# Two of sixteen expert weights loaded as 24, 24 and 80 rows, with an eight-row transfer ahead of the first two parts

## The chip, the cores and the metric

The kernel runs on one core of one Trainium2 chip. A core has a matrix engine (PE, with its weight loads shown apart as PEld), a vector engine (DVE), a scalar engine (ACT), a general engine (POOL, GpSimd) and a queue engine (SP), and sixteen DMA engines that move data between the device memory and the core's own memory of 128 partitions (rows). The metric is the device time of one execution in microseconds, as the median of several runs. Lower is better.

## The reference

The reference is an attention layer, followed by a soft mixture of experts over its output. Batch is 4, heads are 8, the sequence is 768, a head has 64 columns. Three heads see the whole causal triangle, five see four sink positions and a window of 64.

```python
scores = np.where(mask, scale * q @ k.T, -1e9)
attn   = softmax(scores) @ v                    # 4 x 8 x 768 x 64
x      = attn.transpose(0, 2, 1, 3).reshape(3072, 512)

logits     = x @ phi                            # 3072 x 32
d          = softmax over the 3072 rows (logits)
slot_input = (d.T @ x).reshape(8, 4, 512)
for e in range(8):
    h = np.maximum(slot_input[e] @ w1[e], 0.0)  # w1[e] is 512 x 1024
    slot_out[e] = h @ w2[e]                     # w2[e] is 1024 x 512
c   = softmax over the 32 slots (logits)
out = c @ slot_out                              # 3072 x 512, float32
```

All inputs are float32. The sixteen weights (eight `w1`, eight `w2`) are 2.1 MB each, so 33.6 MB of the 52.5 MB that the kernel reads are weights.

## The kernel before, in words

The kernel keeps everything in bfloat16 on the core. Every load is a DMA that POOL issues and that casts float32 to bfloat16 on the way. `dma()` (line 329) makes each of them: it enters an "issue" operation for POOL and a "land" operation into a plan, puts every issue behind the one before it (`fifo`), and lets the issue of a transfer wait for the landing of the transfer eight places earlier (`chain[-8]`). A planner (`Plan`) then orders all operations on all engines by keys, tuned shifts and estimated durations, and the program is emitted in that order. POOL does little else than issue these loads: it makes tables at the start, copies `elg` once for each of three batches (line 801), and issues the first output stores (line 1017).

The loads go in this order: q, k and v of batch 0 in two parts each, with weight 0 behind them; q, k, v of batch 1; weights 1, 2; q, k, v of batch 2; weights 3, 4, 5; q, k, v of batch 3; weights 6 to 10; and last weights 11 to 15 into memory that the attention no longer needs. Weights 0 to 7 are `w1` of the experts, 8 to 15 are `w2`. A weight is a tile of 128 rows, 16 KB of float32 to a row; `load_w` (line 385) loads it in one transfer. The loads of q, k and v have 96 rows. Weights 14 and 15 come in two halves of their columns each (`load_half`, line 381), so that the left half of the output can start before the right halves are there. A slot of memory (`slots`, eleven of them) has to come free before the next load into it is issued; PE frees one by transposing a q, k or v.

Meanwhile PE, ACT and DVE run the attention: transposes (line 566), scores (line 599), exponentials on ACT (line 668), masks on DVE (line 615), the product with v (line 729). After it come the experts: the first product (`H`, line 904), a transpose (line 926), the second product (`W2`, line 942), and the output (`OM`, line 998; scaled on ACT and DVE in lines 1006 and 1008), stored by `store` (line 1017): the left halves of the first three row groups by POOL, all else by SP.

Before the first data are there, PE multiplies zeros: `zeros` (line 482) issues six matmuls of the tile `zt` (128 x 448) into a scores buffer, twice.

Of the kernel before, what the change touches and what calls it, by code (L numbers as in the profile page):

```python
# [11 lines left out]
BF16 = mybir.dt.bfloat16  # L12
# [3 lines left out]
PSUM = bass.MemoryType.PSUM  # L16
KB = 512
PAD = 16


class Buf:
# [130 lines left out]
def pe(ns, n=1):  # L152
    occ = ns * n / 1000.0
    return {"PE": (occ, occ + 0.27)}
# [61 lines left out]
def kernel(  # L216
# [13 lines left out]
    nc = tc.nc  # L230
    P = 128
# [3 lines left out]
    NS = moe_phi.shape[1]  # L235
# [4 lines left out]
    sb = ctx.enter_context(tc.tile_pool(name="sb", bufs=1))  # L240
# [4 lines left out]

    slots = [sb.tile([P, 8 * KB + 2 * PAD], BF16, name=f"slot{i}") for i in range(11)]
    qk_mem = [sb.tile([P, 12 * KB], BF16, name=f"qk{i}") for i in range(2)]
# [18 lines left out]
    rs = [sb.tile([P, 2, 6], F32, name=f"rs{i}") for i in range(2)]  # L266
    rrow = sb.tile([P, 24], F32, name="rrow")
    sum4 = sb.tile([P, NS], BF16, name="sum4")
    zt = sb.tile([P, 448], BF16, name="zt")
    emask = sb.tile([P, 2], F32, name="emask")  # L270
    rcs = sb.tile([P, 1], F32, name="rcs")
    cols = sb.tile([P, 1], BF16, name="cols")
# [18 lines left out]
    scb = [ps.tile([P, 2, 512], F32, name=f"sc{i}") for i in range(2)]  # L291
# [23 lines left out]
    def on(eng, occ, late=0.18):  # L315
        return {eng: (occ, occ + late)}
# [12 lines left out]
    def dma(name, nbytes, buf, dst, src, deps=()):  # L329
        if len(chain) >= 8:  # L330
            deps = list(deps) + [chain[-8]]
        iss = pl.op("issue " + name, on("POOL", 0.645, 1.4), -100, deps=list(deps) + [fifo[0]],
                    acq=[buf] if buf else [], lead=1.3, emit=lambda o: nc.gpsimd.dma_start(dst(), src))  # L333
        fifo[0] = iss
        took = nbytes / 425000.0
        chain.append(pl.op("land " + name, {"DMA": (took, took + 1.3 + min(2.1, 0.22 * len(chain)))}, -100, deps=[iss] + chain[-1:], lead=3.4))
        return chain[-1]
# [25 lines left out]
    wbuf = [Buf("S8") for _ in range(NW)]  # L363
    wland = [None] * NW
    late_mem = {}

    def w_mem(i):

        m = late_mem[i]() if i in late_mem else slots[wbuf[i].slot][:, :]
        return m.rearrange("p (h x) -> p h x", h=2)[:, :, 0:4 * KB]  # L370
# [14 lines left out]
    def load_w(i, deps=()):  # L385
        if i < NE:
            src = moe_w1[i].rearrange("(di h a) f -> di h (a f)", h=2, a=2)
        else:
            src = moe_w2[i - NE].rearrange("(fi h a) d -> fi h (a d)", h=2, a=4)
        wland[i] = dma(f"w{i}", 2 << 20, None if i in late_mem else wbuf[i],  # L390
                       lambda: w_mem(i), src, deps=deps)


    def tables(o):
# [32 lines left out]
    def head_flags(o, n):  # L427
        cp = nc.scalar.copy if o.eng == "ACT" else nc.gpsimd.tensor_copy
        for a, j0, j1 in ((1, 1, 4), (0, 0, 1)):
            cp(fmx[:, n, :, j0:j1, :].rearrange("p i j d -> p i (j d)"),  # L430
               thr[:, a, n::4].rearrange("p (i o) -> p i o", o=1).to_broadcast([P, 2, 66 * (j1 - j0)]))
# [48 lines left out]
    zfb = Buf("SC")  # L480

    def zeros(name, n, key, dep, took=0.43):
        def emit_z(o):
            for _ in range(n):
                nc.tensor.matmul(scb[zfb.slot][:, 0, 0:448], zt[:, 0:128], zt, start=True, stop=True)  # L485

        return pl.op(name, pe(1000 * took, n), key, deps=dep, acq=[zfb] if name == "ZF0" else [], rel=[zfb],
                     emit=emit_z, mode="full", mm=n)
# [15 lines left out]
    for n in range(4):  # L504
        o_fm[n] = pl.op(f"fm{n}", on("ACT", 0.65) if n == 0 else on("POOL", 0.9), -8 if n == 0 else T * n - 3.5,
                        deps=[o_fl], emit=lambda o, n=n: head_flags(o, n))
# [5 lines left out]
    def batch_loads(b):  # L512
        for x in "qkv":
            load_part(x, b)

    load_w(0)
    batch_loads(1)
    load_w(1)
    load_w(2)
    batch_loads(2)  # L520
    for i in (3, 4, 5):
# [67 lines left out]
    def evs(x, b, n):  # L589
        return ev[x, 0, n // 2] if b == 0 else ev[x, b]  # L590
# [15 lines left out]
    def mask_emit(b, n, g):  # L606
        def f(o):
            pT = pTs[PTb[b, n].slot]
            mh = msk[:, n::4, :]
            if g < 2:  # L610
                pT = pT[:, :, 1024 * g:1024 * (g + 1)].rearrange("p i (a c) -> p i a c", a=2)[:, :, :, 0:256]
                mh = mh[:, :, 256 * g:256 * g + 512].rearrange("p i (a c) -> p i a c", a=2)
            else:
                pT, mh = pT[:, :, 2048:2432], mh[:, :, 256:640]
            nc.vector.tensor_tensor(pT, pT, mh, op=ALU.mult)  # L615
        return f
# [5 lines left out]
    for b in range(B):  # L622
        for n in range(4):
# [29 lines left out]
            for kk, g in enumerate(range(5)):  # L653
# [19 lines left out]
                for m, gs in enumerate(MGROUPS):  # L673
                    if gs[-1] == g:
                        o_m = pl.op(f"MK.{p}.{m}", on("DVE", [0.605, 0.605, 0.47][m]), key + 0.3,
                                    deps=[expo[p, x] for x in gs] + [o_hm[n]], emit=mask_emit(b, n, m))
# [3 lines left out]
        for ns in ([(0, 1), (2, 3)] if b == 0 else [(0, 1, 2, 3)]):  # L680
            sc = Buf("SC")

            def emit_lx(o, b=b, sc=sc, ns=ns):
# [4 lines left out]
                      deps=list(dict.fromkeys(e for n in ns for x in "qk" for e in evs(x, b, n))),  # L688
# [14 lines left out]
    for b in range(B):  # L703
        for n in range(4):
# [5 lines left out]
            for i in iorder:  # L710
                deps, need = [v2e[p], vfo[p]], set()
# [7 lines left out]
                def emit_pv(o, b=b, n=n, p=p, i=i):  # L719
                    pT = pTs[PTb[b, n].slot]  # L720
                    vb = vbs[VBb[b].slot]
                    for h in range(2):
                        for j in range(i + 1):
# [3 lines left out]
                            else:  # L727
# [5 lines left out]
                             deps=list(dict.fromkeys(deps)) + ([last] if last else []),  # L733
# [8 lines left out]
            for i0, i1 in halves:  # L742
                part = f"{p}" if i1 - i0 == 6 else f"{p}.{i0}"

                def emit_nm(o, i0=i0, i1=i1, b=b, n=n, p=p):
# [9 lines left out]
                                 deps=[pvo[i1 - 1], XBb[b].op], acq=[XBb[b]] if n == 0 else [], rel=[PVb[p]],  # L755
# [94 lines left out]

    late_mem[11] = lambda: qk_mem[QTb[2].slot][:, 0:8 * KB + 2 * PAD]
    late_mem[12] = lambda: vx_mem[VBb[2].slot][:, 0:8 * KB + 2 * PAD]
    late_mem[13] = lambda: xv_mem[:, 0:8 * KB + 2 * PAD]
    late_mem[14] = lambda: pt_mem[:, 10 * KB * PTb[3, 2].slot:10 * KB * PTb[3, 2].slot + 8 * KB]
# [233 lines left out]
```

## Time and profile before

| what | value |
|---|---|
| median of 3 runs | 151.17 us (150.8 to 151.35) |
| the profiled execution's own time | 150.88 us |
| its span, first to last instruction | 149.1 us, so 1.78 us lie around the span |
| PE busy | 125.5 us (84%) |
| DVE busy | 109.1 us (73%) |
| ACT busy | 107.4 us (72%) |
| POOL busy | 33.1 us (22%) |
| software DMA queue (POOL's), share of 16 engines' span | 95.0% |
| read from and written to device memory | 52.50 MB and 6.29 MB |
| weights and inputs issued by POOL, one issue | 629 to 891 ns on POOL |
| last load issued, landed | 108.43 us, 131.52 us |
| granted PE clock, mean | 0.935 |

The page of the profile shows busy times by engine, then the span cut into 40 slices with a digit of busy tenths in each; the row DMA there is the mean over the sixteen DMA engines, and GB/s counts bytes as they are written on the core, so a load that casts from float32 reads twice that. The chain of waits goes back from the last instruction, step by step, to what released it. A stretch (a window of time) gives busy times, granted clock, DMA share and GB/s of that window alone; the packets there overlap a little, so that the DMA share of a full window comes out over 1. Beside these views, the trace holds for each transfer sixteen marks of its completion, one from each DMA engine, with their times; they tell how far apart the engines are, and carry no engine's number.

### The profile page before, as it was taken

How to read it: one execution, taken by the hardware profiler on the slowest of the kernel's cores; microseconds unless marked ns; L12 is line 12 of the kernel's file. 1: busy time of each engine (PE TensorE's matmuls, PEld its weight loads, DVE VectorE, ACT ScalarE, POOL GpSimd, SP SyncE). 2: the span in 40 equal slices, each digit the busy share in tenths (PEclk: the TensorE clock that was granted, in tenths of full speed). 3: DMA queues.
4: the chain of work that ended last, by engine and by line, in shares of the span. 5: the costliest groups of instructions: out<-in, count | busy, mean ns of one | idle time of the engine just before them, and what ended most of it. 6: DMA issues, size and time to landing. Idle time of an engine off the chain costs nothing.

```text
span 149.1 us, 5309 instructions
## 1 busy us (share of the span) xinstructions
PE 125.5 (84%) x2351; PEld 85.8 (58%) x2351; DVE 109.1 (73%) x232; ACT 107.4 (72%) x138; POOL 33.1 (22%) x58
## 2 busy tenths in 40 slices
PE   6799987996999999999999997999779994959100
PEld 1297665774776776877667775757565552634000
DVE  1897999966898988999899997998953130749500
ACT  3127899996779999999999997999913530738300
POOL 6996301111111001210210122050630000430000
PEclk9999999999599999999999999999968999586975
DMA  2999999999999999999999999999999999999995
GB/s 21 193 210 210 216 214 215 216 214 213 216 210 215 215 216 218 209 212 218 214 216 212 211 216 219 216 211 212 213 220 215 201 196 198 142 305 336 391 422 209
DMA packets 14263, 32.92 MB, mean 221 GB/s; under 512 B 1376, under 2 KB 7008, under 8 KB 13856
## 3 DMA queue, kind: packets, MB, share of 16 engines
q0 software_dynamic: 11536, 27.79, 95.0%
q1 hardware_dynamic: 2704, 4.79, 8.5%
q8 instruction: 18, 0.29, 0.7%
q14 instruction: 5, 0.04, 0.1%
HBM read 52.50 MB, written 6.29 MB: 394 GB/s over the span
## 4 chain that ended last, share of the span: by engine, by line
PE 48%; DMA 15%; DVE 11%; ACT 8%; issue 7%; POOL 3%; DVEq 1%; POOLq 0%; ACTq 0%
DMA qk<-in_moe_w_dram 15%; PE tr L566 13%; PE sc L599 11%; PE pv L729 11%; ACT pt L668 5%; PE tr L762 3%; PE bk L998 3%; DVE xv L750 2%; PE tr L632 2%; DVE pt L615 2%; PE sc L485 2%; DVE vx L322 1%; ACT qk L320 1%; DVE slot L1008 1%; DVE vf L647 1%
## 5 line engine op out<-in xcount | busy, mean ns | idle before, releaser
L668 ACT ACTIVATE pt<-sc 128x1024 bf16<-128x1024 f32 x80 | 77.4, 1047 | 4.9 <-PE sc L599 4.6
L599 PE MATMUL sc<-qk 64*128 64x128 bf16 (+3 forms) x288 | 32.1, 298 | 1.6 <-ACT pt L668 1.4
L615 DVE TENSOR_TENSOR pt<-pt,msk 128x1024 bf16<-128x1024 bf16 (+1 forms) x48 | 30.1, 639 | 1.5 <-ACT pt L668 1.1
L729 PEld LDWEIGHTS <-pt 128*128 128x128 bf16 x640 | 23.9, 98 | 6.8 <-issue 3.7
L729 PE MATMUL pv<-vx,pt 128*128 128x65 bf16 x352 | 26.9, 194 | 0.1
L566 PEld LDWEIGHTS <-slot 96*64 96x64 bf16 x768 | 20.1, 115 | 7.2 <-issue 5.3
L729 PE MATMUL pv<-vf,pt 128*128 128x65 bf16 x288 | 21.7, 196 | 0.9 <-DVE xv L750 0.9
L566 PE MATMUL tr<-ident,slot 96*64 96x96 bf16 x576 | 18.0, 212 | 1.3 <-issue 1.3
L322 DVE COPY qk<-tr 128x768 bf16<-128x768 bf16 x28 | 14.9, 549 | 4.0 <-PE tr L566 3.9
L599 PEld LDWEIGHTS <-qk 64*128 64x128 bf16 x288 | 11.5, 95 | 9.0 <-issue 3.3
L750 DVE TENSOR_TENSOR xv<-pv,rs 128x768 bf16<-128x768 f32 (+1 forms) x17 | 15.5, 910 | 0.6
L333 POOL DMA_DIRECT2D slot<-in_moe_w_dram x11 | 7.8, 707 | 26.6 <-PE tr L566 19.2
L1006 ACT ACTIVATE slot<-bk,rrow 128x256 f32<-128x256 f32 (+1 forms) x17 | 8.5, 548 | 3.6 <-PE bk L998 3.5
L762 PE MATMUL tr<-ident,xv 128*128 128x128 bf16 x96 | 8.8, 230 | 1.4 <-DVE xv L750 0.9
L1008 DVE TENSOR_SCALAR slot<-bk,rrow 128x256 f32<-128x256 f32 (+1 forms) x19 | 9.3, 561 | 0.6 <-PE bk L998 0.4
L762 PEld LDWEIGHTS <-xv 128*128 128x128 bf16 x96 | 6.2, 102 | 4.9 <-DVE xv L750 2.5
L632 PE MATMUL tr<-ident,xv 128*128 128x128 bf16 x96 | 8.2, 220 | 1.0 <-issue 0.9
L322 DVE COPY xT<-tr 128x768 bf16<-128x768 bf16 (+1 forms) x14 | 7.3, 525 | 2.3 <-PE tr L762 1.3
L998 PE MATMUL bk<-msk,expT 128*128 128x256 bf16 (+1 forms) x36 | 8.4, 413 | 0.7 <-DVE msk L983 0.7
L322 DVE COPY vx<-tr 128x768 bf16<-128x768 bf16 x13 | 7.1, 550 | 1.1 <-PE tr L632 1.0
L632 PEld LDWEIGHTS <-xv 128*128 128x128 bf16 x96 | 5.7, 97 | 3.0 <-issue 2.5
L1017 POOL DMA_DIRECT2D out_dram<-slot x4 | 2.8, 709 | 19.6 <-DVE slot L1008 19.5
(101 smaller groups left out, 152.1 us busy)
## 6 DMA issues: line engine op xcount, KB each, us to landing
slot<-in_moe_w_dram POOLq DMA_DIRECT2D x11, 1024.0 KB, 26.4
out_dram<-slot SPq DMA_DIRECT2D x3, 1024.0 KB, 6.6
slot<-in_q_dram POOLq DMA_DIRECT2D x3, 768.0 KB, 30.4
slot<-in_k_dram POOLq DMA_DIRECT2D x3, 768.0 KB, 32.7
slot<-in_v_dram POOLq DMA_DIRECT2D x3, 768.0 KB, 23.8
out_dram<-slot SPq DMA_DIRECT2D x3, 512.0 KB, 3.7
qk<-in_moe_w_dram POOLq DMA_DIRECT2D x1, 1024.0 KB, 21.3
vx<-in_moe_w_dram POOLq DMA_DIRECT2D x1, 1024.0 KB, 24.0
```

The lines of the kernel that those rows point to most:

```text
L322: nc.vector.tensor_copy(dst, src)
L566: nc.tensor.transpose(dst_, rv[:, i, 8 * c + s, :], idv)
L599: nc.tensor.matmul(scb[sc.slot][:, i, c:c + 128 * nb], kk, qq.rearrange("p b c -> p (b c)"), start=True, stop=True)
L615: nc.vector.tensor_tensor(pT, pT, mh, op=ALU.mult)
L632: nc.tensor.transpose(t[:, 128 * j:128 * (j + 1)], vT[:, 6 * n + j, :], ident)
L668: nc.scalar.activation(pTs[PTb[b, n].slot][:, :, 512 * g:512 * (g + 1)], scb[sc.slot], ACT.Exp, scale=scale)
L729: nc.tensor.matmul(pvb[:, h, 65 * i:65 * (i + 1)], lt, rhs, start=(j == 0), stop=(j == i))
L750: nc.vector.tensor_tensor(xo, pvw[:, :, :, 0:64], r.rearrange("p i (j o) -> p i j o", o=1).to_broadcast([P, 2, i1 - i0, 64]), op=ALU.mult)
L762: nc.tensor.transpose(t[:, 128 * i:128 * (i + 1)], xv[:, i, 128 * n:128 * (n + 1)], ident)
L998: nc.tensor.matmul(banks[bf.slot][:, 0:w], out_lhs(gi, r), slot_out[:, cs], start=True, stop=True)
L1006: nc.scalar.activation(d, banks[bf.slot][:, 0:w], ACT.Copy, scale=sc_)
L1008: nc.vector.tensor_scalar(d, banks[bf.slot][:, 0:w], sc_, None, op0=ALU.mult)
```

## The change

Weights 6 and 7 (the `w1` of experts 6 and 7) are no longer loaded in one transfer of 128 rows. Each is loaded in three: rows 0 to 23, rows 24 to 47, and rows 48 to 127. In front of each of the two small parts stands a transfer of eight rows of `moe_phi` (128 bytes each, cast to 64) into a new tile `few` that nothing reads. So each of the two weights becomes five transfers in the order 8, 24, 8, 24, 80 rows. The bytes of the weights are the same. The tile `zt` shrinks from 448 to 416 columns, which gives the 64 bytes to a row that `few` takes, and the zero matmuls write 416 columns. No other load, and no operation of the other engines, is edited; the order of PE, DVE and ACT stays as it was, and on POOL the `elg` copy that stood behind the issues of weights 6 and 7 now stands between the two.

```diff
+UNEVEN = {6: (0, 24, 0, 24, 80), 7: (0, 24, 0, 24, 80)}
...
-    zt = sb.tile([P, 448], BF16, name="zt")
+    zt = sb.tile([P, 416], BF16, name="zt")
+    few = sb.tile([8, NS], BF16, name="few")
...
     def load_w(i, deps=()):
...
-        wland[i] = dma(f"w{i}", 2 << 20, None if i in late_mem else wbuf[i],
-                       lambda: w_mem(i), src, deps=deps)
+        if i not in UNEVEN:
+            wland[i] = dma(f"w{i}", 2 << 20, None if i in late_mem else wbuf[i],
+                           lambda: w_mem(i), src, deps=deps)
+            return
+        rows, p0 = UNEVEN[i], 0
+        for x, n in enumerate(rows):
+            if n == 0:
+                dma(f"gap{i}.{x}", 1024, None, lambda: few, moe_phi[0:8, :])
+                continue
+            wland[i] = dma(f"w{i}.{p0}", n << 14, wbuf[i] if p0 == 0 else None,
+                           lambda p0=p0, n=n: w_mem(i)[p0:p0 + n], src[p0:p0 + n], deps=deps)
+            p0 += n
+        assert p0 == 128
...
-                nc.tensor.matmul(scb[zfb.slot][:, 0, 0:448], zt[:, 0:128], zt, start=True, stop=True)
+                nc.tensor.matmul(scb[zfb.slot][:, 0, 0:416], zt[:, 0:128], zt, start=True, stop=True)
```

## The prediction

> **What bounds the kernel now.** I read the page first (which resource is full), then the chain of waits at its end (what releases the last work), then stretches around that point (what the DMA engines do there), and POOL's timeline (what could hold the changed transfers up).
>
> ```profile
> DMA  2999999999999999999999999999999999999995
> q0 software_dynamic: 11536, 27.79, 95.0%
> q8 instruction: 18, 0.29, 0.7%
> ```
>
> The DMA engines are full from the second slice to the next to last: reading 33.6 MB of weights and 18.9 MB of q, k, v is what the time consists of. The queue of instruction fetches carries little, 18 packets, but each goes to one engine only.
>
> ```profile
> 107.56 0.86 POOL pt L333
> 108.43 23.09 DMA qk<-in_moe_w_dram
> 131.52 0.04 issue
> 131.56 0.43 PE bk L942 x8
> 132.09 0.49 DVE msk L983
> 132.63 3.91 PE bk L998 x16
> ```
>
> The last half weight is issued at 108.43 and lands at 131.52; PE goes on 0.04 us later. From there to the end of the span 17.6 us follow (second product, output, stores), so a landing that moves by x moves the end by x, as long as the half before it (weight 15, left) moves too, which releases the first stores.
>
> ```profile
> 124.00:126.00 2.00, 0.27 (x12) 0.09 (x1) 0.00 (x0) 0.00 (x0) 0.00 (x0) 1.00 1.45 197
> 127.60:128.00 0.40, 0.40 (x3) 0.30 (x2) 0.31 (x1) 0.00 (x0) 0.00 (x0) 0.50 0.77 102
> 128.00:128.80 0.80, 0.80 (x6) 0.58 (x4) 0.79 (x2) 0.74 (x2) 0.01 (x1) 0.50 0.80 102
> 128.90:129.90 1.00, 1.00 (x6) 0.59 (x4) 1.00 (x3) 1.00 (x4) 0.90 (x2) 0.53 0.65 89
> ```
>
> The last two columns are DMA share and GB/s. From 127.6 on the rate is half (102 against 197): half of the engines have finished while the others still load. The sixteen completion marks say the same:
>
> | transfer | earlier eight engines, us | later eight, us |
> |---|---|---|
> | weight 6 | 82.72 to 83.44 | 83.94 to 85.60 |
> | weight 15, left half | 122.30 to 122.69, and 123.53 | 124.68 to 125.22, and 126.25 |
> | weight 15, right half | 127.62 to 128.00, and 128.85 | 129.94 to 130.49, then 131.20 and 131.52 |
>
> The lag grows one engine at a time: after each instruction fetch (893 to 974 ns a packet, every 6 us or so) one more engine lands late, until eight are late after the eighth; then the first of them get a second. 18 fetches over eight engines are two each and three for two of them, which is 1.9 us and 2.9 us: the 2.2 and 3.3 to 3.5 us seen. So eight engines are free of fetches, and between the two groups there are about 2.3 us to share out.
>
> **The change part by part.**
>
> *A row's price.* Weight 6 to weight 7, one engine's first mark moves from 82.72 to 87.61: 4.89 us for eight rows, 0.61 us a row. The 96-row loads give 3.71 us for six (74.16 to 77.87), 0.62: the shape does not matter. Weights 6 and 7 together are 16 rows an engine, 9.8 us. Only how the rows are dealt can move the end; which is what the trace does not show, since all its POOL loads have 96 or 128 rows and go evenly to sixteen engines. I bound it by four deals of 24 rows, each with 80 rows as five to an engine:
>
> 1. Equal shares, two rows to twelve engines, each transfer starting where the last one stopped. In one weight eight engines get two shares (5 + 4 = 9 rows) and eight get one (7). But a weight moves the starting point by 12 + 12 = 24, or 40 if the eight-row transfers move it by eight too; both are 8 modulo 16. So the second weight gives nine rows to those that got seven: 16 for every engine, as before. Gain 0.
> 2. Row by row over sixteen engines, start moved by eight by each small transfer: always the same eight get 2 + 2 + 5 = 9, twice. They gain two rows (+1.22 us), the others lose two (-1.22).
> 3. Three rows to eight engines, the same eight each time: 11 against 5, twice, so +3.67 and -3.67 us.
> 4. Two rows to the same twelve engines each time: 18 rows for twelve (+1.22), 10 for four (-3.67).
>
> The trace speaks for equal shares (six and eight rows to each engine; fourteen marks of weight 0, before most fetches, lie within 0.63 us, 20.26 to 20.89); twelve is the largest number of engines up to sixteen that 24 rows allow, and sixteen is what 96 and 128 rows get, also the largest. I take deal 1. The Trainium skill, "DMA: Bandwidth & Descriptors", section "Why a DMA increments its semaphore by 16 and not by 1", has this as a rule: the largest count up to 16 that divides the slowest dimensions of both sides, on consecutive engines from a round-robin cursor. No run here shows it for 24 rows; by it the sum is deal 1. The same section measured an exception, sixteen shares rounded up on always the same engines, by which the sum would be deal 4.
>
> *Eight more transfers.* Their bytes are nothing; what they add on a ring is the completion and, on eight engines, one packet of 64 bytes, four times. Lower bound: a weight takes 4.90 us, its 16 packets, which start 0.305 us apart, 4.88, so 0.02 us a transfer, 0.16 for eight. Upper bound: the slowest completion packets (0.08 us) and the 0.06 us that packets of 512 bytes take: 8 x 0.08 + 4 x 0.06 = 0.9 us. I take 0.2, near the lower, because it comes from the same queue at full load. A reason for less than nothing I see none. The same page, section "Anatomy of one DMA", gives a fixed 2 us a transfer; eight of them in a row would be 16 us by that. The trace disagrees as far as the ring is concerned: transfers follow each other in 0.02 us, the rest is hidden by the transfer ahead.
>
> *POOL and the wait for the eighth transfer back.*
>
> ```profile
> 59.25 0.63 POOL L333 DMA_DIRECT2D slot<-in_v_dram  x1 [10.85 <-PE tr L566]
> 59.87 0.70 POOL L333 DMA_DIRECT2D slot<-in_moe_w_dram  x1
> 64.09 0.71 POOL L333 DMA_DIRECT2D slot<-in_moe_w_dram  x1 [3.51 <-PE tr L566]
> 71.71 0.83 POOL L801 COPY elg<-elg 128x576 bf16<-128x576 bf16 x1 [6.91 <-DMA slot<-in_q_dram]
> 77.26 0.70 POOL L333 DMA_DIRECT2D slot<-in_moe_w_dram  x1 [4.72 <-DMA slot<-in_k_dram]
> 82.74 0.71 POOL L333 DMA_DIRECT2D slot<-in_moe_w_dram  x1 [4.78 <-PE tr L566]
> ```
>
> Eight issues of some 0.65 us are 5.2 us more on POOL (22% busy). But each issue waits for the eighth landing before it, and small transfers use up places. Counting: the 80 rows of weight 6 wait for weight 5 (69.67, ahead of the `elg` copy at 71.71, which is therefore not late); weight 7's first 24 rows for k of batch 3 (77.00); its second small transfer for v of batch 3 (80.68); the next two follow by 82.7, and weight 8 about 83.4 instead of 77.26. An issue turns into data about 1.6 us later (a store issued at 128.79 has its first mark at 130.73, 0.37 us of it data), so weight 7's 80 rows are at hand by 84.3 and weight 8 by 85.0. The earliest engine is through weight 6 at 82.72 and needs weight 8 at 87.6. An early engine without a share in weight 7's first part can stand idle up to 1.6 us; it has 2.3 us in hand, the late engines (85.60) never wait. Cost 0; with the cover gone (issues 2.3 us later still) the excess counts in full. Weights 9 to 15 wait for transfers landed long before, or for PE as now. The experts' waits for more parts (weights 6 and 7, used from 119.66) are met 25 us earlier.
>
> *Smaller zeros.* Twelve matmuls of 0.39 us (six took 2.35 us) lose 32 of 448 columns: 12 x 0.028 = 0.34 us less PE before the first transposes. PE does not set the end, the loads do: 0. If it did, at most -0.34.
>
> *Sum.* 0 for the rows, +0.2 for the transfers, 0 else: 150.88 + 0.2 = 151.1 for an execution like the profiled one, which lies 0.29 under the median; on the median 151.17 + 0.2 = 151.4.
>
> **The rivals.**
>
> *The free eight get more (deal 2, or another that gives them two rows).* For it: the lag is 2.3 us, a shift of 1.22 on both sides would close it almost exactly. Early engines would end at 128.84 to 129.22 and 130.07, late ones at 128.72 to 130.30. The last landing moves from 131.52 to 130.30, that of weight 15's left half from 126.25 to 125.03 (early ones: 124.75 at most): -1.2 + 0.2, so 150.2. Against it: it needs a deal in unequal shares, or a start that returns, and the right eight of the sixteen. It turns into no gain at a shift of 2.7 us, where the early ones reach 131.5.
>
> *A lopsided deal that ends late.* Deal 3 on the free eight: 128.85 + 3.67 = 132.52, +1.0 and 0.2: 152.4. Deal 2 on the eight that fetch, or deal 4 with the slowest among its twelve: 131.52 + 1.22 + 0.2, so 152.6. Deal 3 on the wrong eight: +3.9, 155.0. For it: nothing in the profile says which engines fetch. Against: equal shares, as above.
>
> *The queue runs dry* because POOL stands behind a landing: each us over the 2.3 in hand counts; 2 us over would be 153.4. Against it: weight 8's data are at hand 2.6 us before they are needed (85.0 and 87.6).
>
> **How the numbers follow.** Deal 1 (the change does not do what it says over the two weights): 0.45, alone 150.9 to 152.0. The free eight gain: 0.25. Lopsided and late: 0.25. Dry queue: 0.05. A measurement tells about 0.5% (0.75 us) from no change. Faster takes the second case, less a little for a smaller gain: 0.24. Same takes the first, less its upper end: 0.45. Slower the rest: 0.31. The range runs from a little under the gain's 150.2 to deal 4's 152.6; wrong-side deal 3, dry queue and edges stay outside.
>
> **What would show it.** Right: the marks of the last landing again in two groups 2 us apart, the rate halved for some 2 us ahead of it, the last landing at 131.5 to 131.9; after weight 6 alone, eight engines moved by 0.6 us, and moved back after weight 7. Gain: one cluster within 1.6 us, no stretch at 100 GB/s. Lopsided: marks of weight 7 spread over 4 us or more. Wrong in the waits: a gap in the DMA row around 83 to 88 us, POOL waiting there for a landing.

## The result, and the profile after

The changed kernel takes **159.62 us** (158.59 to 160.86, four runs) against 151.0 us (150.8 to 151.35, four runs): ratio 1.057, 95% interval 1.047 to 1.067, so 8.6 us slower. The forecast was 151.4 with a range of 150.0 to 152.6. The profiled execution is the slowest of the four (160.86 us, span 159.1, so 10.0 over the span before).

The page of the kernel before has these rows by slices of 3.7 us:

```profile
PE   6799987996999999999999997999779994959100
PEclk9999999999599999999999999999968999586975
```

The page of the changed kernel, by slices of 4 us:

```profile
PE   5899987997999999995009999999995999986000
PEclk9999999999999999999555579999999999999555
DMA  3999999999999999999919389999999999979994
q0 software_dynamic: 11792, 27.79, 90.1%
```

The DMA row, full before from the second slice on, now has a 1 (79.5 to 83.5 us) and a 3 (87.5 to 91.5 us). PE stands still for two slices, and the granted clock is at half for four slices in a row. The bytes of q0 are the same 27.79 MB, its share fell from 95.0% of 149.1 us to 90.1% of 159.1 us, which is 141.6 and 143.3 us. So only 1.7 of the 10.0 us are more work for the DMA engines, at most; the rest is time in which they had nothing to do. Three stretches (busy time of PE, PEld, DVE, ACT and POOL, clock, DMA share, GB/s) put bounds on it, first in the changed kernel:

```profile
81.00:82.00 1.00, 0.00 (x0) 0.00 (x0) 0.00 (x0) 0.00 (x0) 1.00 (x2) 0.50 0.00 0
...
72.00:82.00 10.00, 1.62 (x29) 0.77 (x25) 3.06 (x6) 1.93 (x3) 1.03 (x2) 0.70 0.79 158
82.00:92.00 10.00, 8.55 (x113) 5.58 (x114) 4.46 (x8) 5.58 (x7) 4.37 (x9) 0.50 0.62 109
```

The last two before:

```profile
72.00:82.00 10.00, 9.89 (x224) 6.74 (x224) 9.52 (x19) 9.58 (x12) 1.24 (x2) 1.00 1.07 215
82.00:92.00 10.00, 9.09 (x202) 6.65 (x202) 9.51 (x19) 9.63 (x12) 2.80 (x4) 1.00 1.07 215
```

Both ran at 215 GB/s. Now 57 and 106 GB/s are missing, which is 2.7 and 4.9 us of a full queue, and another 0.7 us goes missing by 93 us (66 GB/s): 8.3 us. The last landing moved by nearly that, from 131.52 to 139.63 (+8.1).

POOL's timeline says who kept the queue empty (start, duration, line, what is issued; in brackets the idle time ahead and what ended it):

```profile
60.02 0.53 POOL L335 DMA_DIRECT2D few<-in_moe_phi_dram  x1
...
80.97 0.53 POOL L335 DMA_DIRECT2D few<-in_moe_phi_dram  x1 [19.79 <-DMA few<-in_moe_phi_dram]
81.49 1.24 POOL L335 DMA_DIRECT2D slot<-in_moe_w_dram  x2
82.72 0.68 POOL L814 COPY elg<-elg 128x576 bf16<-128x576 bf16 x1
83.33 0.52 POOL L335 DMA_DIRECT2D few<-in_moe_phi_dram  x1
83.84 0.62 POOL L335 DMA_DIRECT2D slot<-in_moe_w_dram  x1
89.96 0.53 POOL L335 DMA_DIRECT2D few<-in_moe_phi_dram  x1 [5.49 <-DMA few<-in_moe_phi_dram]
90.48 2.08 POOL L335 DMA_DIRECT2D slot<-in_moe_w_dram  x3
```

All four small transfers write the same tile `few`. No line of the diff asks for a wait between them; it comes with the shared tile, and the profile lists it (`few` waits for the DMA of `few`). So the second may not be issued before the first has landed; the first, issued at 60.02, lands only at 80.68, because every engine takes it up behind the q, k and v of batch 3 that were queued before it: v's sixteen marks run from 77.93 to 80.53, those of the small transfer from 78.10 to 80.68, each 0.15 to 0.2 us behind one of v's. For 20 us POOL stands in front of that wait, and with it all that it has yet to issue. By the time it goes on, the rings hold nothing. At the fourth small transfer it happens again: it waits for the third (landed 88.25 to 89.68), which is queued behind the 80 rows of weight 6 (88.05 to 89.48).

The `elg` copy (line 814, 801 before) is on the same queue: it starts at 82.72, before at 71.71. The list of waits between 70 and 95 us has the two in one chain:

```profile
POOL few L335 <- DMA few<-in_moe_phi_dram: 25.3, 2, 19.8
...
PE tr L849 <- POOL elg L814: 9.8, 1, 9.8
```

PE needs `elg` for the six transposes of line 849, which come next in its order: it stops for 9.8 us. The chain of waits shows the same order of events:

```profile
60.02 20.66 DMA few<-in_moe_phi_dram
...
82.72 0.69 POOL elg L814
...
83.45 0.82 PE tr L849 x6
```

So one wait has two effects, both of the size of the loss: empty rings (8.1 us on the last landing), and a PE that stands still (9.8 us). Which of them makes the end late the profile alone does not decide: the left half of the output starts 1.9 us after its weight has landed (136.28 and 134.36), so there PE is the later; the right half starts 0.04 us after its weight (139.67 and 139.63), so there the load is.

### The profile page after: what moved, and what is told of

Its sections match the earlier page's. It is cut to its first block, busy times and chain, and to the rows that moved or that the text cites. A ratio compares the mean times of both kernels' runs of the same rounds, so it can differ in the third digit from the quotient of the medians.

```text
span 159.1 us, 5321 instructions
## 1 busy us (share of the span) xinstructions
PE 126.2 (79%) x2351; PEld 86.8 (55%) x2351; DVE 109.1 (69%) x232; ACT 106.8 (67%) x138; POOL 37.2 (23%) x66
## 3 DMA queue, kind: packets, MB, share of 16 engines
q0 software_dynamic: 11792, 27.79, 90.1%
## 4 chain that ended last, share of the span: by engine, by line
PE 44%; ACT 14%; DMA 13%; DVE 10%; issue 7%; POOL 4%; DVEq 0%; POOLq 0%; ACTq 0%
DMA few<-in_moe_phi_dram 13%; PE tr L579 12%; ACT pt L681 11%; PE sc L612 8%; PE pv L742 7%; PE bk L1011 3%; DVE slot L1021 3%; PE bk L917 2%; PE bk L955 2%; PE tr L775 2%; POOL slot L335 2%; PE pv L509 2%; DVE pt L628 2%; PE sc L498 1%; DVE vx L324 1%
## 5 line engine op out<-in xcount | busy, mean ns | idle before, releaser
L612 PE MATMUL sc<-qk 64*128 64x128 bf16 (+3 forms) x288 | 33.0, 303 | 2.2 <-ACT pt L681 2.0
L742 PEld LDWEIGHTS <-pt 128*128 128x128 bf16 x640 | 24.4, 99 | 7.5 <-issue 4.2
L579 PEld LDWEIGHTS <-slot 96*64 96x64 bf16 x768 | 21.2, 121 | 7.1 <-issue 5.8
L335 POOL DMA_DIRECT2D slot<-in_moe_w_dram x15 | 10.1, 675 | 19.7 <-PE tr L579 13.5
L856 ACT ACTIVATE expT<-tr 128x768 bf16<-128x768 bf16 x4 | 3.4, 844 | 11.0 <-PE tr L849 11.0
L849 PE MATMUL tr<-ident_r,elg 128*128 128x128 bf16 x24 | 2.3, 243 | 9.8 <-POOL elg L814 9.8
L1019 ACT ACTIVATE slot<-bk,rrow 128x256 f32<-128x256 f32 (+1 forms) x17 | 7.7, 571 | 1.7 <-PE bk L1011 1.7
L775 PEld LDWEIGHTS <-xv 128*128 128x128 bf16 x96 | 6.0, 100 | 4.8 <-issue 2.1
L335 POOL DMA_DIRECT2D few<-in_moe_phi_dram x4 | 2.1, 530 | 25.3 <-DMA few<-in_moe_phi_dram 25.3
L579 PE MATMUL tr<-ident_u,slot 96*64 96x96 bf16 x192 | 7.5, 245 | 0.1
```

What stands on the lines that cost most here:

```text
L579: nc.tensor.transpose(dst_, rv[:, i, 8 * c + s, :], idv)
L612: nc.tensor.matmul(scb[sc.slot][:, i, c:c + 128 * nb], kk, qq.rearrange("p b c -> p (b c)"), start=True, stop=True)
L742: nc.tensor.matmul(pvb[:, h, 65 * i:65 * (i + 1)], lt, rhs, start=(j == 0), stop=(j == i))
L775: nc.tensor.transpose(t[:, 128 * i:128 * (i + 1)], xv[:, i, 128 * n:128 * (n + 1)], ident)
L1019: nc.scalar.activation(d, banks[bf.slot][:, 0:w], ACT.Copy, scale=sc_)
```

## The experiments

All the kernels below compute the whole of the reference; nothing reads what the small transfers bring. Line numbers of a variant may differ from those of the changed kernel by one; the kernel with the repeated copy has those of the kernel before.

**Is it the one tile?** The changed kernel with a tile for each small transfer:

```diff
-    few = sb.tile([8, NS], BF16, name="few")
+    fews = [sb.tile([8, NS], BF16, name=f"few{i}") for i in range(4)]
...
-                dma(f"gap{i}.{x}", 1024, None, lambda: few, moe_phi[0:8, :])
+                dma(f"gap{i}.{x}", 1024, None, lambda i=i, x=x: fews[2 * (i - 6) + x // 2], moe_phi[0:8, :])
```

(The zeros' tile has 320 columns here, to make room.)

> The changed kernel, but each of the four small transfers writes a tile of its own (the zero tile shrinks to 320 columns for them), so that none waits for another. If the loss comes from the small transfers waiting for each other through their one tile: back to 151.0 to 151.8 us, no dry stretch in the DMA row. If it comes from cutting the weights into 24, 24 and 80 rows, or from the waits for the eighth transfer back: 156 us or more.

Measured 151.73 us (151.27 to 152.81; ratio 1.0049, interval 1.0026 to 1.0072). 7.9 of the 8.6 us are gone with the reuse of the tile alone. POOL's waits are now for landings eight places back, as the prediction had counted, and for PE, and the copy runs on time:

```profile
69.80 0.61 POOL L335 DMA_DIRECT2D slot<-in_moe_w_dram  x1 [4.61 <-DMA slot<-in_moe_w_dram]
70.41 0.94 POOL L814 COPY elg<-elg 128x576 bf16<-128x576 bf16 x1
...
81.73 0.53 POOL L335 DMA_DIRECT2D few<-in_moe_phi_dram  x1 [2.87 <-DMA slot<-in_v_dram]
```

What is left of the change is 0.7 us. In the profiled execution, a slow one of the ten (152.81 us), the rate dips between 84 and 88 us (191 GB/s; before 213), which is 0.4 us of a full queue; the second and third part of weight 7 are issued only at 82.25 and 82.87, which fits, but was not tried by itself. So the 0.7 us are the cost of eight more transfers and of these late issues together, and no run here parts the two.

**Are the small transfers enough, without the cut?** Weights 6 and 7 whole again, and the four small transfers on one tile in front of them:

```diff
-UNEVEN = {6: (0, 24, 0, 24, 80), 7: (0, 24, 0, 24, 80)}
+UNEVEN = {6: (0, 0, 128), 7: (0, 0, 128)}
```

> Weights 6 and 7 whole, with two small transfers into one tile in front of each: the waits without the cut. If the waits make the loss: the second small transfer is issued at 80.7 to 81.0, the fourth about 88, each with a dry stretch behind it, and POOL's copy of elg comes about 88.7, so that 158 to 165 us. If the cut makes the loss: 151 to 152 us.

Measured 168.85 us (167.65 and 170.04; ratio 1.117, interval 1.107 to 1.127), worse than the change itself and above the 158 to 165 us that were expected: here the `elg` copy stands behind the fourth small transfer and starts at 90.48. Both waits grew:

```profile
POOL few L335 <- DMA few<-in_moe_phi_dram: 30.1, 3, 22.8
...
PE tr L849 <- POOL elg L814: 20.1, 1, 20.1
```

So the cut into parts is not the cause. Together with the first experiment, and with the cut alone (below, 151.32), this places the loss in the reuse of the tile.

**Dry rings alone.** The `elg` copy goes ahead of the second small transfer, so PE gets it on time, and all waits on `few` stay:

```diff
+    pv_ops["issue gap6.2"].deps.append(pv_ops["EL4.1"])
```

> The changed kernel with POOL's copy of elg put ahead of the second small transfer, so that PE is not held up by it, while the small transfers wait for each other as before. If the dry DMA rings alone are enough for the loss: last load about 139.6, 157 to 160 us. If PE's stop of 9.8 us behind the late copy makes the loss and the rings do not: 151 to 153 us.

Measured 158.45 us (157.59 to 158.62; ratio 1.048, interval 1.044 to 1.051). The copy starts at 70.62, and PE works through the same stretches at full clock, while the DMA share is nearly as low as in the changed kernel:

```profile
72.00:82.00 10.00, 9.41 (x223) 6.60 (x219) 9.16 (x17) 9.06 (x12) 0.80 (x2) 1.00 0.79 159
82.00:92.00 10.00, 9.69 (x206) 7.22 (x201) 9.58 (x20) 9.75 (x12) 4.82 (x9) 1.00 0.69 118
```

The last weight lands at 138.63 (+7.1), and PE now waits for weights at the end. Empty rings alone cost 7.4 us.

**PE's stop alone.** The kernel before, with its `elg` copy of batch 1 repeated thirteen times, so that PE gets it late while the loads stay:

```diff
-... emit=lambda o, b=b: nc.gpsimd.tensor_copy(
-                elg[:, b % 2, :, 1:4], elg[:, b % 2, :, 0:1].to_broadcast([P, 6, 3, NS])))
+... emit=lambda o, b=b: [nc.gpsimd.tensor_copy(
+                elg[:, b % 2, :, 1:4], elg[:, b % 2, :, 0:1].to_broadcast([P, 6, 3, NS])) for _ in range(13 if b == 1 else 1)])
```

> The kernel before, with POOL's second copy of elg made thirteen times over, so that it ends about 10 us late while all loads are issued in time: PE's stop without dry rings. If PE's stop alone is enough: PE has 2.0 us in hand ahead of weight 15's left half, 9.8 - 2.0 = 7.8 us, so about 158 to 159 us. If the rings alone make the loss: 151 to 152 us.

Measured 158.18 us (157.07 to 158.91; ratio 1.046, interval 1.041 to 1.051). The waits, and the same two stretches:

```profile
PE tr L836 <- POOL elg L801: 8.3, 1, 8.3
```

```profile
72.00:82.00 10.00, 1.69 (x26) 1.10 (x20) 2.14 (x4) 1.07 (x3) 8.24 (x13) 0.68 1.06 214
82.00:92.00 10.00, 10.00 (x174) 6.74 (x172) 6.25 (x12) 7.22 (x9) 0.70 (x1) 0.64 0.95 179
```

The loads run on at 214 GB/s through the stop, and thin out only after it (179), since PE has not freed the slot that weight 8 needs (issued at 87.52, before at 77.26). The last landing is 134.28, 5.35 us ahead of the changed kernel's, and PE waits for no weight at the end. So PE's stop alone, here 8.3 us long, costs 7.15 us. The isolation is not perfect, as the late weight 8 shows; but without a wait for a weight the loads do not set the end.

The two effects do not add up: 7.4 and 7.15 us apart, 8.6 together. They are two parallel ways to the end, and the longer one hides the other. PE's stop in the changed kernel is 9.8 us, 1.5 longer than with the repeated copy; with these 1.5 added to the 7.15, PE's way alone would come to about 8.7 us, the whole of the loss (an estimate from these two runs). Undoing PE's stop alone, as the kernel with the copy ahead does, gained only 1.2 us of the 8.6.

PE's way can be followed at its own instructions. The `elg` transposes come at 73.01 before and 83.45 after (+10.4). The last transposes of the attention come at 112.50 and 124.81 (+12.3); the half clock after the stop is the likely reason for the 1.9 us more. In the kernel before, PE then waits 3.2 us for the last weights (2.0 of it at one time):

```profile
PE bk L942 <- DMA qk<-in_moe_w_dram: 3.2, 2, 2.0
```

In the changed kernel these waits are gone. That leaves 9.1 of the 10.0 us of the two profiled spans. For the kernel with the repeated copy the same count gives 9.8 - 3.2 = 6.6 of 7.5. What the rest is, 0.9 us in both, stays open.

**The cut alone**, with no small transfer:

```diff
-UNEVEN = {6: (0, 24, 0, 24, 80), 7: (0, 24, 0, 24, 80)}
+UNEVEN = {6: (24, 24, 80), 7: (24, 24, 80)}
```

> Weights 6 and 7 in 24, 24 and 80 rows without any small transfer. If 24 rows go as two rows to twelve engines, and each transfer starts where the last one stopped, the second weight undoes what the first one shifts: the end as before, 150.8 to 151.6 us, eight early and eight late marks about 2 us apart at the last landing. If the start does not move: the same engines get more both times, and the last landing moves by 1 us or more, 150.2 or 152.2 us.

Measured 151.32 us (150.68 to 152.2; ratio 1.001, interval 0.9991 to 1.0029). The marks of the last landing lie in the same two groups as before: 127.63 to 128.85 and 129.88 to 131.67. So over two weights the rows come out even. In the changed kernel the marks show how 24 rows are dealt, since there the rings are empty ahead of them and all engines start together: the second part of weight 6 has four marks at 83.10 to 83.14 and twelve at 84.99 to 85.35, the second part of weight 7 four at 92.06 to 92.78 and twelve at 94.07 to 94.68. So four engines get nothing, and twelve get two rows each. This agrees with the rule of the Trainium skill, "DMA: Bandwidth & Descriptors", section "Why a DMA increments its semaphore by 16 and not by 1" (the largest count up to 16 that divides both sides, on consecutive engines from a cursor that moves on). The exception named there, sixteen shares rounded up, would also leave four engines out. What speaks against it is the cut alone: with the same four left out each time, the prediction's deal 4, their marks would come 3.67 us earlier after two weights, and no mark at the last landing does (the first is at 127.63, before at 127.62).

**Can the intended gain be had?** By that rule, one start moved by eight between the two weights would give the same eight engines nine rows in both. One small transfer alone, ahead of weight 7, does this without any tile used twice (the zeros' tile has 384 columns here, and 320 in the next three):

```diff
-UNEVEN = {6: (0, 24, 0, 24, 80), 7: (0, 24, 0, 24, 80)}
+UNEVEN = {6: (24, 24, 80), 7: (0, 24, 24, 80)}
...
-    few = sb.tile([8, NS], BF16, name="few")
+    few = sb.tile([8, 2, NS], BF16, name="few")
...
-                dma(f"gap{i}.{x}", 1024, None, lambda: few, moe_phi[0:8, :])
+                dma(f"gap{i}.{x}", 1024, None, lambda: few[:, :, 0:NS // 2], moe_phi[0:8, :].rearrange("p (h x) -> p h x", h=2))
```

> As the run without small transfers, but one eight-row transfer stands between weights 6 and 7, with two pieces to a row so that its rows go to eight engines in turn and move the start by eight: the same eight engines then get nine rows of both weights. If the start moves as the equal-shares deal has it, this run or its twin with one more small transfer in front (the other eight) comes out 0.8 to 1.2 us faster (150.0 to 150.3 us) with one cluster of marks at the end, and the other of the two 0.6 to 1.4 us slower. If the start does not move so: both about 151.2 us.

The next one has a small transfer ahead of weight 6 as well, with a tile of its own, which moves the chosen eight to the other eight (`UNEVEN = {6: (0, 24, 24, 80), 7: (0, 24, 24, 80)}`):

> The twin: one more small transfer, into a tile of its own, in front of weight 6, so that the other eight engines get nine rows of both weights. If the deal is as said: 150.0 to 150.3 us where the run with one small transfer is slower, 151.6 to 152.6 us where that one is faster. If not: about 151.2 us.

Two more turn the window by two and by fourteen engines, with a small transfer of two or fourteen rows far ahead, in front of weight 3 (a negative number is the count of its rows), and with the copy of `elg` kept ahead of weight 7:

```diff
+UNEVEN = {3: (-2, 128), 6: (24, 24, 80), 7: (-8, 24, 24, 80)}
...
+    pv_ops["issue w7.0"].deps.append(pv_ops["EL4.1"])
```

> As the run in which the same eight engines get nine rows of both weights, with one more small transfer of two rows far ahead (in front of weight 3), which moves the start on by two engines; the copy of elg stands ahead of weight 7's parts. At the end of that run two engines lay at 126.6 to 127.0 us and two or three at 131.1 to 131.7, as if six of its eight were free of fetches and two were not, so that the window is off by two, one way or the other. If so, this run or its twin has all of the late landings within 130.3 us and takes 150.0 to 150.5 us, and the other one has four of eight right, and takes 151.3 to 152.5 us. If the window is not what matters: both about 151.3 us.

> The twin with a small transfer of fourteen rows instead of two, which moves the start on by fourteen, that is, back by two. 150.0 to 150.5 us where the run with two rows takes 151.3 to 152.5 us, and the other way round; both about 151.3 us if the window is not what matters.

| small transfers | time, us (ratio, interval) | marks of the last landing, us |
|---|---|---|
| none, cut only | 151.32 (0.9991 to 1.0029) | 127.63 to 128.85; 129.88 to 131.67 |
| 8 rows ahead of 7 | 151.28 (0.9987 to 1.0028) | two at 126.62, 127.01; eleven at 128.88 to 130.12; 130.77, 131.12, 131.65 |
| 8 rows ahead of 6 and of 7 | 152.56 (1.0067 to 1.0116) | six at 127.35 to 128.32; four at 129.12 to 129.41; six at 131.45 to 132.80 |
| 2 ahead of 3, 8 ahead of 7 | 151.27 (0.9981 to 1.0027) | three at 126.85 to 127.02; ten at 128.96 to 130.33; three at 131.55 to 131.76 |
| 14 ahead of 3, 8 ahead of 7 | 152.51 (1.0056 to 1.0127) | two at 127.03, 127.45; twelve at 128.97 to 130.25; two at 131.92, 132.63 |

The ratios are against the kernel before in the same series (151.19 us, and 151.45 for the last two rows).

Shares do move: in three of the four, ten to twelve marks come together in one cluster of at most 1.4 us, where before there were two groups. But in each of these two or three marks come early and two or three late, as engines without fetches that are left short and engines with fetches that get more would give, and the last mark sets the end. None of the four is faster than the kernel before. The second kernel is slower by about what two rows cost (1.37 us; two rows are 1.22), as one of the first pair was expected to be, but its twin did not gain. For the last two the expectation was missed altogether: turning the window by two, one way or the other, was to bring all late marks within 130.3 us in one of them, and in both some came at 131.5 or later. So nothing shows that the fetch-free eight are consecutive engines at all. The marks carry no engine's number; whether another choice would give the 1.2 us stays open.

**The zeros.** The smaller tile `zt` alone, with both weights whole (`UNEVEN = {}`):

> Only the zero tile shrinks to 416 columns, all loads as before. By every theory of the loads no change, 150.8 to 151.3 us; if the shorter warm-up cost PE its clock, 152 us or more.

Measured 151.19 us against 151.19 (ratio 1.000, interval 0.998 to 1.0019): nothing. The 320 columns of some kernels above were not tried alone, but one of them takes 151.27 us against 151.45.

## Why the prediction was wrong

*What bounds the kernel* held: a late last landing makes a late end (+7.1 us of landing, +7.4 us of time where PE was kept on time). It lacked a second bound close behind: PE waits only 3.2 us for the last weights, so anything that stops PE for longer decides as well.

*A row's price and the deal* held as far as the marks show. Twelve engines get two rows each, and two weights even each other out (the cut alone, 151.32). The step's 0 is what was measured.

*Eight more transfers* was taken at 0.2. With four tiles 0.7 was measured, but that holds the late issues of weight 7 too: the queue did not stay quite full (191 GB/s at 84 to 88 us, worth 0.4 us), and the lower bound came from a queue at full load. So part of the miss probably belongs to the next step, and the 0.2 itself was not measured alone. (The upper bound of 0.9 took 0.08 us for the slowest completion packet; the trace has 0.09, which makes it 1.0.)

*POOL and the wait for the eighth transfer back* is the step that failed. It counted one kind of wait, the one eight places back, and dated every issue by it: the second small transfer of weight 7 by v of batch 3, weight 8 at 83.4. It left out that the four small transfers write one tile, so that each also waits for the landing of the one before. The transfer's 1 KB made it look as if it were done at once; it was done 20.66 us after its issue, because that is how long the queue ahead of it was. All the figures for it were in the trace of before: v of batch 3 lands at 80.68, so the second small transfer could be issued at 80.7 and no earlier. "Cost 0" became 7.9 of the 8.6 us. With that wait taken out, the step's dates were good to about 1 us: with four tiles the second small transfer of weight 7 waits for v of batch 3, as counted, and is issued at 81.73 (its landing counted at 80.68), and the next two follow at 82.25 and 82.87 (counted by 82.7).

In the same step stood the sentence that the `elg` copy "is therefore not late". It was 11.0 us late, for the same reason, and PE stopped 9.8 us behind it. The prediction asked what is queued behind the waiting issue, and asked it of the wrong wait.

*Smaller zeros* at 0: confirmed.

*The rivals.* The dry queue, 0.05, is what came, but through another wait than the one it was given for, and four times as large as its worked case of 2 us (153.4). The sign listed for it, a gap in the DMA row around 83 to 88 us with POOL waiting for a landing, came as two gaps on either side of that time (0.25 and 0.30 of the DMA engines' time at 80 to 84 and 88 to 92 us, 1.03 between). Of the lopsided deals, "deal 2 on the eight that fetch" at 152.6 has a near relative among the runs: the kernel with small transfers ahead of both weights came to 152.56, though its marks have six late engines, not eight. The free eight's gain (150.2) was not reached by any window.

## What to carry to other kernels

Before an added transfer is called free, list every wait of its issue, the reuse of its destination among them: a filler that nothing reads still needs a tile of its own, because a tiny transfer lands no sooner than the queue ahead of it (here 20.66 us after its issue), and all that its issuing engine has yet to do waits with it. If that engine also makes a copy for another engine, a DMA wait becomes a stop of that engine, so ask of each wait which queues stand behind it. And where one cause opens two ways to be late, undo them one at a time and both together: here one alone gave back 1.2 us, and both 7.9.

## What was not expected of the hardware

*The clock after a stop.* After 9.8 us without work PE's granted clock stayed at 0.50 long after work had begun again. Two stretches of the changed kernel:

```profile
92.00:93.00 1.00, 1.00 (x22) 1.00 (x20) 0.04 (x1) 0.29 (x1) 0.56 (x1) 0.50 0.46 66
93.00:94.00 1.00, 1.00 (x21) 0.49 (x20) 0.67 (x2) 0.37 (x1) 0.00 (x0) 0.93 1.02 201
```

Work began at 83.45 and the clock rose at about 93.1, 9.7 us later. With the repeated copy it took 8.2 us (81.03 to 89.2). In the kernel with uncut weights, after a stop of twice the length, it took only 3.7 us (91.22 to 94.9). The Trainium skill, "TensorE: Matmul & The Clock Gate", Part 1, names about 3.4 us of sustained work; only the last of the three agrees. In the three traces' records of the clock, the stretches at half last 17.07, 13.65 and 20.48 us, that is 5, 4 and 6 times 3.41 us; so the clock changed only on a grid of 3.41 us. In the third kernel the first whole step of that grid after the restart was enough. In the other two it took two whole steps, though the profile has PE busy throughout in all of them (58, 46 and 42 matmuls in the first whole step, in the order above). What held the clock down there was not tested.

*The engines are level after empty rings.* The second small transfer, issued into empty rings, has its sixteen marks within 0.21 us (82.40 to 82.61), while the small one before it, behind a full queue, has them spread over 2.6 us (78.10 to 80.68). So the engines' standing lag was gone once the queue had run empty. It grew back: at the last landing the marks again span 2.6 us (137.00 to 139.63).
